# Gated linear attention, a maximum layer and a top-1 expert layer in one kernel: one block's matmuls moved a slice ahead, small copies moved to another queue, preparations and routings moved in the written order

## The chip, the cores and the metric

One core of a Trainium2 chip. The time is that of one execution on the device, in microseconds (us). The engines are named as in the profile: PE (TensorE, matmuls), PEld (its weight loads), DVE (VectorE), ACT (ScalarE), POOL (GpSimd), SP (SyncE, which here only issues DMAs). A name with q (ACTq, SPq) is the engine's sequencer, for example while it issues a DMA.

## The reference

```python
def _attn_ref(q, k, v, alpha):            # 4 batches, 8 heads, 768 steps, head size 48
    for t in range(S):
        state = alpha[:, :, t, :, None] * state + einsum('bhd,bhe->bhde', k[:, :, t], v[:, :, t])
        y[:, :, t] = einsum('bhd,bhde->bhe', q[:, :, t], state)

def _moe_ref(x, w1, w2, w3, w_out):       # x: 3072 x 384, hidden size 768
    h = maximum(maximum(x @ w1, x @ w2), x @ w3)
    return h @ w_out

def _moe2_ref(x, w_gate, w_output_gate, w1, w2):   # 8 experts, hidden size 1024
    e_idx = argmax(x @ w_gate, axis=1)
    for e in range(8):                    # each token goes through one expert
        ye = maximum(x[mask] @ w1[e], 0) @ w2[e]
        out[mask] = gate_w[mask] * sigmoid(x[mask] @ w_output_gate)[:, e] * ye
```

The three functions run one after the other: attention, maximum layer, expert layer.

## The kernel before

**Blocks.** The 3072 tokens are worked in 8 blocks of 384 (two to a batch). A block's attention is cut into 3 chunks of 128 steps and 2 groups b of heads, so 6 attention steps, written (chunk, b). `attend(old, new)` (L276 to L340) does the second half of one step and the first half of the next one. On PE it issues L288 (y from q and the carried state), L297 (transposes of k), L304 (y from the scores A and v), L310 (the update X of the state) and L317 (the scores of the next step). X and y share the one PSUM tile of pool `psY`. DVE then adds X to the state (L325, L327) and masks the scores into A (L338). ACT copies the transposed k (`kn`, L299), scales the next group's state (L330) and copies y into the tile `x32` (L335); only then can the next step's L288 write to `psY`. L304 of that step waits for A.

**Preparation.** Before a block's attention DVE turns its decays into products: `prep_z` (a scan, L191), `prep_k` (L196), `prep_p` (L203 to L208, with a second scan) and `prep_q` (L212), once for each b; one tile Z serves them in turn. `check` and `check_pl` are activations on ACT that look for decays outside the expected range (L175, L177).

**From attention to the maximum layer.** After chunk 2 of b = 1, `finish_x` (L342) moves the fourth head pair's rows to where they belong by six small DMAs from SBUF to SBUF, all issued by ACT. When b = 0 is done too, `split_x` (L348) cuts x into a high and a low part: xH by ACT (L352), xL by DVE (L353), one column block k = 0, 1, 2 after the other. The weights come as packed 64-bit words by SP (`fetch`, L370) and are cut likewise: `cast_a` is three DVE passes (L393, L395, L397), `cast_b` three ACT copies to wH (L405), `cast_c` one DVE subtraction to wL (L409). A cast of number n (0 to 5) makes one slice f = n of 128 hidden columns for the three matrices; n = 6 and 7 make the two halves of the output weights.

**The maximum layer.** `mm1(i, f, w)` (L435) is block i, slice f, matrix w: nine matmuls into one of three PSUM banks of pool `psM`, the products wH·xH, wH·xL and wL·xH for each k. ACT copies the first bank (L444), DVE takes the maximum of the other two (L447, L450), ACT casts the result (L461) and `mm1_lo` takes the low part (L466). `mm2` (L468) is the second product, and `gate_a`, `gate_b` (L411, L419) fold the routing weights into the output weights by transposes (PE), copies (ACT) and small matmuls (PE, then L429 on ACT, L430 on DVE).

**Routing.** `route_a` (L507) finds each token's expert on DVE; `route_b` (L531) counts by two small matmuls, which read its results `oh` and `oc`, into the one bank of pool `psO`; `route_c` and `route_d` (L539, L559) are chains of small DVE operations that read that bank. `mm2` of the blocks from 2 on uses the same bank.

**Order.** Each engine works its own instructions in program order, and that order is written by hand: each `on(t, f, ...)` or `seq(t, dt, ...)` places a function at a time t in units of about one `mm1`, and all are sorted by t. The start (L995 to L1017) is a list with everything up to slice 0 of block 0. Then a list of `steps` places slices of block 0 and block 1 in turn (L1020 to L1044): (0,0), (1,0), (0,1), (1,1), ... with the remaining casts, the gates and block 2's preparation between them. `seq(30, ...)` places block 2's attention among the `mm2` of blocks 0 and 1; block 2's maximum layer begins at 36, block 3's attention at 42, block 4's at 51, block 3's maximum layer at 54. `warm_up(n)` (L950) is n matmuls of a constant that nobody reads. The expert layer follows at the end and is untouched.

Of the kernel before, what the change touches and what calls it, by code (L numbers as in the profile page):

```python
# [88 lines left out]
def _layers(ctx, tc, pool_, wk, K, general, qk, al, a0, v, vT, w123, wout, gates, ew1, ew2, out):  # L89
# [880 lines left out]
    if not general:  # L970
        batches = [(c, b) for c in range(CPB) for b in (1, 0)]

        def last(i, x, y=None):

            def f():
                attend(x and (i, *x), y and (i, *y))
                if x == (2, 1):
                    finish_x(i)
            return (f,)

        def cross(i, x, j, y):

            def f():
                attend((i, *x), (j, *y))
                if x == (2, 1):
                    finish_x(i)
            return (f,)

        def cast_in(n):
# [16 lines left out]
            cross(1, (0, 1), 0, (2, 0)), (warm_up, 4), *ca[:2],  # L1006
            cross(0, (2, 0), 1, (1, 1)), (warm_up, 4), ca[2],
            last(1, (1, 1), (0, 0)), (warm_up, 4), *ch_,
            last(1, (0, 0), (2, 1)), (warm_up, 4), (split_x, 0), cl,
            last(1, (2, 1), (1, 0)), *da[:2], (mm1, 0, 0, 0),  # L1010
            last(1, (1, 0), (2, 0)), da[2], (mm1, 0, 0, 1),
            last(1, (2, 0)), *dh, (mm1, 0, 0, 2), (mm1_lo, 0, 0), (split_x, 1), dl, (load_qkv, 2), (route_consts,))


        steps = []
        for n in (2, 3, 4, 5, 6, 7):
            wa, wh, wl = cast_in(n)  # L1017
# [1 line left out]
            steps += [[[wa[0]], [wa[1]], []], [[wa[2], *nxt, *wh], [wl], []]]
        wa, wh, wl = cast_in(7)  # L1020
        steps[9][2] = [wa[0]]
        steps[10:] = [[[wa[1]], [wa[2], *wh], [(prep_z, 2, 1)]], [[wl], [(prep_k, 2, 1)], [(check_pl, 2), (prep_p, 2, 1)]]]
# [4 lines left out]
        for n, w, fs in ((9, 2, [ga[0]]), (10, 0, [ga[1]]), (10, 1, [gb[0]]), (10, 2, [ga[2], gb[1]]), (11, 0, [gb[2]]),  # L1027
                         (11, 1, [ga[3]]), (11, 2, [ga[4], gb[3]])):
            steps[n][w] = fs + steps[n][w]
        p = []  # L1030
# [245 lines left out]
```

## Time and profile before

| what | value |
|---|---|
| median of 3 runs | 760.96 us (758.26 to 762.04) |
| the profiled execution's own time | 760.24 us |
| its span, first to last instruction | 758.5 us |
| mean granted clock of PE | 0.985 of full |
| instructions | 14575 |

The profiled execution is the one all rows come from. Its own time is 1.7 us above its span, and 0.72 us below the median. Start times in the rows are counted from the start of the span. "Busy" is the time in which an engine has an instruction under way; "idle before" names what ended the wait.

### The profile page before, as it was taken

The numbers are of one execution on the slowest core, as the hardware profiler recorded it, in microseconds if no ns is written. First come the engines' busy times: TensorE is split into PE (matmuls) and PEld (weight loads), VectorE is DVE, ScalarE is ACT, GpSimd is POOL, SyncE is SP. The second block draws the span as 40 slices with busy tenths as digits, with TensorE's granted clock in tenths as the row PEclk, the third lists the DMA queues.
The fourth block names the chain that finished last, engine by engine and source line by source line (L and its number), as shares of the span: only waits on it lengthen the run. The fifth ranks groups of instructions, "written<-read, shape, count | busy, mean of one in ns | idle before, by whom it ended". The sixth has DMA issues, their size and how long they took to land. (4 is left out here: it accounts for less than half of the span.)

```text
span 758.5 us, 14575 instructions
## 1 busy us (share of the span) xinstructions
PE 717.1 (95%) x4782; PEld 637.3 (84%) x4782; DVE 380.8 (50%) x803; ACT 305.9 (40%) x750; POOL 110.6 (15%) x117
## 2 busy tenths in 40 slices
PE   7799999998999999999999999899999999999994
PEld 7688998897999998999999997789975789984672
DVE  7877787468866736637233266411113531111533
ACT  4354433554543524434222234333335553333743
POOL 1000000011021211111111120222222222222211
PEclk9999999999899999999999999999999999999998
DMA  9805210561410412300000041111279631169770
GB/s 265 338 17 177 81 64 1 163 153 46 124 44 28 130 40 55 97 22 10 12 22 9 31 188 32 43 43 44 65 276 336 225 123 40 45 218 385 284 267 23
DMA packets 23741, 86.57 MB, mean 114 GB/s; under 512 B 7988, under 2 KB 11852, under 8 KB 19536
## 3 DMA queue, kind: packets, MB, share of 16 engines
q1 hardware_dynamic: 18192, 73.24, 28.9%
q0 software_dynamic: 3904, 10.84, 4.4%
q10 hardware_dynamic: 1536, 1.18, 0.6%
q8 instruction: 51, 0.84, 0.5%
q14 instruction: 58, 0.48, 0.2%
HBM read 128.09 MB, written 10.63 MB: 183 GB/s over the span
## 5 line engine op out<-in xcount | busy, mean ns | idle before, releaser
L440 PE MATMUL hps<-xH,wH 128*128 128x384 f32 x432 | 151.6, 351 | 1.8 <-ACT xH L352 1.8
L440 PE MATMUL hps<-xH,wL 128*128 128x384 f32 x432 | 146.0, 338 | 0.7 <-DVE wL L409 0.7
L440 PE MATMUL hps<-xL,wH 128*128 128x384 f32 x432 | 146.1, 338 | 0.4 <-DVE xL L353 0.4
L466 POOL TENSOR_TENSOR hL<-hm,hH 128x384 fp32r<-128x384 f32 x36 | 44.8, 1244 | 404.6 <-ACT hH L461 404.5
L895 PE MATMUL psP<-w2H,ch 128*128 128x384 f32 x368 | 100.2, 342 | 2.2 <-ACT ch L855 1.4
L836 PE MATMUL psM<-w1H,cx 128*128 128x512 f32 x276 | 97.0, 406 | 1.7 <-ACTq L1180 1.7
L440 PEld LDWEIGHTS hps<-xH,wH 128*128 128x128 f32 x432 | 82.0, 190 | 8.4 <-ACT xH L352 2.5
L856 DVE SCALAR_TENSOR_TENSOR ch<-psH,ch 128x512 fp32r<-128x512 f32 x46 | 29.7, 686 | 109.2 <-ACT ch L855 108.7
L440 PEld LDWEIGHTS hps<-xL,wH 128*128 128x128 f32 x432 | 82.3, 191 | 0.9 <-DVE xL L353 0.9
L440 PEld LDWEIGHTS hps<-xH,wL 128*128 128x128 f32 x432 | 82.1, 190 | 1.0 <-DVE wL L409 1.0
L895 PEld LDWEIGHTS psP<-w2H,ch 128*128 128x128 f32 x368 | 67.1, 188 | 3.2 <-ACT ch L855 1.6
L476 PE MATMUL ops<-wo,hH 128*128 128x400 f32 x258 | 68.2, 345 | 0.0
L836 PEld LDWEIGHTS psM<-w1H,cx 128*128 128x128 f32 x276 | 52.6, 190 | 15.1 <-ACTq L1180 2.0
L895 PE MATMUL psP<-w2L,ch 128*128 128x384 f32 x184 | 62.1, 337 | 0.0
L915 POOL DMA_INDIRECT out<-yo,sidx x30 | 30.9, 1030 | 204.4 <-ACTq L911 117.2
L447 DVE TENSOR_TENSOR hm<-hm,hps 128x384 f32<-128x384 f32 x48 | 26.5, 551 | 66.4 <-PE hps L440 60.8
L836 PE MATMUL psM<-w1L,cx 128*128 128x512 f32 x138 | 54.9, 398 | 0.1
L461 ACT CAST hH<-hm 128x384 fp32r<-128x384 f32 x43 | 22.0, 512 | 80.8 <-DVE hm L450 77.0
L909 ACT ACTIVATE yo<-psP,xg 128x384 f32<-128x384 f32 x30 | 17.5, 582 | 81.5 <-PE psP L895 60.0
L837 ACT COPY hs<-psM 128x512 f32<-128x512 f32 x46 | 27.0, 588 | 56.7 <-PE psM L836 54.6
L476 PEld LDWEIGHTS ops<-wo,hH 128*128 128x128 f32 x258 | 46.9, 188 | 0.4
L476 PE MATMUL ops<-wo,hL 128*128 128x400 f32 x129 | 44.3, 344 | 0.2 <-POOL hL L466 0.2
(211 smaller groups left out, 1159.3 us busy)
## 6 DMA issues: line engine op xcount, KB each, us to landing
s1a<-in_ew SPq DMA_DIRECT2D x15, 1536.0 KB
s2a<-in_ew SPq DMA_DIRECT2D x15, 1536.0 KB
s1b<-in_ew SPq DMA_DIRECT2D x14, 1536.0 KB
s2b<-in_ew SPq DMA_DIRECT2D x14, 1536.0 KB
ws<-in_w SPq DMA_DIRECT2D x6, 1152.0 KB
at<-in_al SPq DMA_DIRECT2D x16, 336.9 KB
vt<-in_v SPq DMA_DIRECT2D x8, 576.0 KB
x2d<-xs SPq DMA_DIRECT2D x24, 192.0 KB
```

The lines of the kernel that those rows point to most:

```text
L440: mm(ps, slab(a, f)[:, w, k], b[i][:, k], start=(n == 0), stop=(n == 8))
L447: nc.vector.tensor_max(m, m, ps)
L461: nc.scalar.copy(hH[i, f], m)
L466: (nc.gpsimd if not general and i > 1 else nc.vector).tensor_sub(hL[i, f], hps["m"], hH[i, f].bitcast(F32))
L476: mm(ps[:, :DM + NG], a[i, f][:, ts_], wo[f // 3][:, b, f % 3], start=(f + n == 0), stop=(f + n == 7))
L836: mm(ps, cx[j][:, x, ks], w[:, k, fs], start=(k + n == 0), stop=(k + n == 4))
L837: nc.scalar.copy(hs[j][:, fs], ps)
L856: nc.vector.scalar_tensor_tensor(lo, ps, 0.0, hi.bitcast(F32), op0=ALU.max, op1=ALU.subtract)
L895: mm(ps[:, :DM], ch[j][:, x, f * 128:(f + 1) * 128], w[:, f], start=(f + n == 0), stop=(f == NE - 1 and n == 2))
L909: nc.scalar.activation(y, ps[:, :DM], AF.Copy, scale=gate)
L915: nc.gpsimd.indirect_dma_start(out=out[:, :], out_offset=bass.IndirectOffsetOnAxis(ap=sidx[:, j:j + 1], axis=0), in_=y, in_offset=None, bo ...
```

## The change

Four groups of edits. (1) `finish_x` of blocks 0 and 1 issues its six DMAs from SP instead of ACT. (2) `mm1` runs its nine matmuls by kind of product (three wH·xH, three wH·xL, three wL·xH) instead of by k. (3) In the start list four `warm_up(4)` are gone, from the step that follows the first step of block 1 on; the first pass of cast 1 stands two attention steps earlier, its second pass behind `mm1(0,0,1)`, its ACT copies ahead of `mm1(0,0,2)`. After that the slices run (0,1), (1,0), (0,2), (1,1), ... (0,5), (1,4), (1,5), so block 0 is a slice ahead; the casts follow each other every four to five `mm1` instead of every six; the gates and block 2's preparation stand earlier. (4) Block 3's preparation moves ahead: `prep_p` and `prep_q` of b = 1 from 38.3 and 39.3 into block 2's last attention step, b = 0 from 42.6 to 45.0 forward to 37.3 to 43.6. The routings of block 0 (45.6 to 46.8) move to 49.7 to 50.9, that of block 1 from 47.4 to 49.2 to 51.5 to 53.9, with 1.2 units instead of 0.6 between `route_a` and `route_b`.

```diff
     def finish_x(i):
         for c in range(3):
             for h in range(2):
-                nc.scalar.dma_start(out=x32[i][64 * h + D:64 * h + 64, c],
+                (nc.sync if i < 2 else nc.scalar).dma_start(out=x32[i][64 * h + D:64 * h + 64, c],
...
-        for k in range(3):
-            for (a, b) in ((wH, xH), (wH, xL), (wL, xH)):
+        for (a, b) in ((wH, xH), (wH, xL), (wL, xH)):
+            for k in range(3):
...
-            cross(1, (0, 1), 0, (2, 0)), (warm_up, 4), *ca[:2],
-            cross(0, (2, 0), 1, (1, 1)), (warm_up, 4), ca[2],
-            last(1, (1, 1), (0, 0)), (warm_up, 4), *ch_,
-            last(1, (0, 0), (2, 1)), (warm_up, 4), (split_x, 0), cl,
-            last(1, (2, 1), (1, 0)), *da[:2], (mm1, 0, 0, 0),
-            last(1, (1, 0), (2, 0)), da[2], (mm1, 0, 0, 1),
-            last(1, (2, 0)), *dh, (mm1, 0, 0, 2), (mm1_lo, 0, 0), (split_x, 1), dl, (load_qkv, 2), (route_consts,))
+            cross(1, (0, 1), 0, (2, 0)), *ca[:2],
+            cross(0, (2, 0), 1, (1, 1)), ca[2],
+            last(1, (1, 1), (0, 0)), *ch_, da[0],
+            last(1, (0, 0), (2, 1)), (split_x, 0), cl,
+            last(1, (2, 1), (1, 0)), (mm1, 0, 0, 0), (mm1, 0, 0, 1), da[1],
+            last(1, (1, 0), (2, 0)), da[2], *dh, (mm1, 0, 0, 2), (mm1_lo, 0, 0),
+            last(1, (2, 0)), dl, (split_x, 1), (load_qkv, 2), (route_consts,))
...
+        order = [(0, 1), (1, 0)]
+        for f in range(2, 6):
+            order += [(0, f), (1, f - 1)]
+        order.append((1, 5))
+        steps = [[[], [], []] for _ in order]
         for n in (2, 3, 4, 5, 6, 7):
...
+            w0 = {2: 0, 3: 5, 4: 10, 5: 14, 6: 19, 7: 23}[n]
+            for m, x in enumerate(([wa[0]], [wa[1]], [wa[2], *nxt, *wh], [wl])):
+                steps[(w0 + m) // 3][(w0 + m) % 3] += x
...
+        for n, w, fs in ((7, 2, [ga[0]]), (8, 0, [ga[1]]), (8, 1, [gb[0]]), (8, 2, [ga[2], gb[1]]), (9, 0, [gb[2]]),
+                         (9, 1, [ga[3]]), (9, 2, [ga[4], gb[3]]), (10, 0, [gb[4]]), (10, 1, [ga[5]]), (10, 2, [gb[5]])):
             steps[n][w] = fs + steps[n][w]
+        for n, w, x in ((9, 1, (prep_z, 2, 1)), (9, 2, (prep_k, 2, 1)), (10, 0, (check_pl, 2)), (10, 0, (prep_p, 2, 1)),
+                        (10, 2, (prep_q, 2, 1))):
+            steps[n][w].append(x)
...
-            (prep_q, 2, 1), gb[4], ga[5], (mm2, 0, 0, lo), gb[5], last(2, None, (0, 1)), (prep_zk, 2, 0), (mm2, 0, 1, lo),
+            (mm2, 0, 0, lo), last(2, None, (0, 1)), (prep_zk, 2, 0), (mm2, 0, 1, lo),
...
-            (mm2, 1, 2, lo), last(2, (2, 0)), (split_x, 2), (mm2, 1, 2, hi), (route_a, 0))
-        seq(37.3, 1, (check_pl, 3), (prep_p, 3, 1), (prep_q, 3, 1), (check, 3, 1, 0), (check, 3, 1, 1))
-        seq(42.6, 0.6, (prep_z, 3, 0), (prep_k, 3, 0), (check, 3, 0, 0), (prep_pq, 3, 0), (check, 3, 0, 1))
-        seq(45.6, 0.6, (route_b, 0), (route_c, 0), (route_d, 0), (route_a, 1), (route_b, 1), (route_c, 1), (route_d, 1))
+            (mm2, 1, 2, lo), (check_pl, 3), (prep_p, 3, 1), last(2, (2, 0)), (split_x, 2), (mm2, 1, 2, hi), (prep_q, 3, 1),
+            (route_a, 0))
+        seq(37.3, 0.9, (prep_z, 3, 0), (check, 3, 1, 0), (prep_k, 3, 0), (check, 3, 1, 1), (prep_p, 3, 0), (check, 3, 0, 0),
+            (prep_q, 3, 0), (check, 3, 0, 1))
+        seq(49.7, 0.6, (route_b, 0), (route_c, 0), (route_d, 0), (route_a, 1))
+        seq(52.7, 0.6, (route_b, 1), (route_c, 1), (route_d, 1))
```

In the lists `ca`, `ch_`, `cl` are the passes of cast 0 on DVE, on ACT and the last on DVE; `da`, `dh`, `dl` those of cast 1. `last` and `cross` are `attend` within a block and across two, with `finish_x` behind (2, 1).

## Rows read from the trace of the kernel before

**Rows 1.** The page, part 1: PE, busy us, share of the span, instructions.
```profile
PE 717.1 (95%) x4782; PEld 637.3 (84%) x4782; DVE 380.8 (50%) x803; ACT 305.9 (40%) x750; POOL 110.6 (15%) x117
```
**Rows 2.** Stretches: busy us of each engine (instructions), granted PE clock, DMA share, GB/s.
```profile
35.60:39.00 3.40, 3.40 (x28) 3.08 (x23) 2.17 (x5) 1.17 (x4) 0.00 (x0) 0.50 0.14 41
39.00:59.40 20.40, 19.62 (x203) 17.08 (x201) 14.22 (x23) 10.99 (x32) 0.00 (x0) 1.00 0.19 49
62.90:66.30 3.40, 3.40 (x13) 3.40 (x12) 3.33 (x3) 0.58 (x3) 0.00 (x0) 0.50 0.12 45
189.20:196.00 6.80, 6.80 (x40) 6.20 (x39) 5.77 (x18) 2.11 (x7) 0.47 (x1) 0.50 0.01 2
```
**Rows 3.** Waits of PE, 20 to 200 us: total us, times, longest us.
```profile
PE rps L534 <- DVE oh L521: 2.5, 1, 2.5
PE hps L440 <- ACT xH L352: 1.8, 2, 1.6
PE y L288 <- ACT x L335: 1.6, 3, 0.6
PE gps L425 <- ACT wT L417: 1.0, 2, 0.7
...
PE hps L440 <- DVE wL L409: 0.7, 1, 0.7
PE XT L297 <- DVE wo L430: 0.5, 1, 0.5
```
**Rows 4.** Timeline of PE, 34 to 51 us: start, us, instruction, idle before it.
```profile
34.28 0.69 PE L288 MATMUL y<-qt,state 112*112 112x128 f32 x4 [2.89 <-DVE pl L208]
...
36.03 1.23 PE L317 MATMUL sc<-qt,kt 48*128 48x128 f32 x8
...
42.38 0.69 PE L288 MATMUL y<-qt,state 112*112 112x128 f32 x4
...
48.51 0.64 PE L288 MATMUL y<-qt,state 112*112 112x128 f32 x4
...
50.50 0.44 PE L440 MATMUL hps<-xH,wH 128*128 128x384 f32 x1
```
**Rows 5.** Timeline of ACT, 28 to 60 us.
```profile
28.00 4.64 ACTq L345 DMA_DIRECT2D x<-x  x6
...
44.94 0.36 ACT L335 COPY x<-y 112x256 f32<-112x256 f32 x1
...
58.75 1.34 ACT L405 CAST wH<-wu 128x384 fp32r<-128x384 f32 x3
```
**Rows 6.** Timeline of DVE, 28 to 36 us.
```profile
30.86 0.51 DVE L327 TENSOR_TENSOR state<-state,y 48x96 f32<-48x96 f32 x2
...
34.24 0.96 DVE L212 TENSOR_TENSOR qt<-qt,Z 112x768 f32<-112x768 f32 x1
```
**Rows 7.** Groups of DVE instructions, 36 to 118 us: count, busy us, mean ns, idle before.
```profile
L395 DVE SCALAR_TENSOR_TENSOR wu<-ws,wu 128x1152 uint32<-128x1152 uint32 x8 | 10.8, 1354 | 0.1
...
L393 DVE TENSOR_SCALAR wu<-ws 128x1152 uint32<-128x1152 uint32 x8 | 6.0, 756 | 0.0
L450 DVE TENSOR_TENSOR hm<-hm,hps 128x384 f32<-128x384 f32 x11 | 6.0, 549 | 2.1 <-PE hps L440 2.1
...
L338 DVE TENSOR_TENSOR A<-sc,mask 128x512 f32<-128x512 f32 x6 | 4.1, 691 | 0.8 <-PE sc L317 0.6
```
**Rows 8.** Timeline of DVE, 153 to 158 us.
```profile
156.08 0.54 DVE L327 TENSOR_TENSOR state<-state,y 48x96 f32<-48x96 f32 x2 [1.53 <-issue]
```
**Rows 9.** Stretches, columns as in Rows 2.
```profile
184.68:185.66 0.98, 0.98 (x7) 0.88 (x5) 0.84 (x8) 0.00 (x0) 0.00 (x0) 1.00 0.07 17
...
202.98:207.77 4.79, 4.79 (x30) 4.76 (x28) 4.76 (x9) 4.56 (x11) 1.02 (x1) 1.00 1.01 323
203.71:207.68 3.97, 3.97 (x25) 3.97 (x24) 3.94 (x8) 3.92 (x10) 1.02 (x1) 1.00 1.01 313
```
**Rows 10.** Timeline of PE, 205 to 211 us.
```profile
208.81 0.71 PE L317 MATMUL sc<-qt,kt 48*128 48x128 f32 x8
```

More of the change, by code (lines that the diff above doesn't have):

```diff
@@ L344, in finish_x @@
             for h in range(2):
-                nc.scalar.dma_start(out=x32[i][64 * h + D:64 * h + 64, c],
-                                    in_=x32[i][64 * h + 16 * c:64 * h + 16 * c + 16, 3])
+                (nc.sync if i < 2 else nc.scalar).dma_start(out=x32[i][64 * h + D:64 * h + 64, c],
+                                                            in_=x32[i][64 * h + 16 * c:64 * h + 16 * c + 16, 3])
     def split_x(i):
@@ L1005, in _layers @@
             cross(0, (1, 0), 1, (0, 1)), (warm_up, 4), (prep_pq, 1, 0),
-            cross(1, (0, 1), 0, (2, 0)), (warm_up, 4), *ca[:2],
-            cross(0, (2, 0), 1, (1, 1)), (warm_up, 4), ca[2],
-            last(1, (1, 1), (0, 0)), (warm_up, 4), *ch_,
-            last(1, (0, 0), (2, 1)), (warm_up, 4), (split_x, 0), cl,
-            last(1, (2, 1), (1, 0)), *da[:2], (mm1, 0, 0, 0),
-            last(1, (1, 0), (2, 0)), da[2], (mm1, 0, 0, 1),
-            last(1, (2, 0)), *dh, (mm1, 0, 0, 2), (mm1_lo, 0, 0), (split_x, 1), dl, (load_qkv, 2), (route_consts,))
-        steps = []
+            cross(1, (0, 1), 0, (2, 0)), *ca[:2],
[10 more added lines that the diff above has]
+        steps = [[[], [], []] for _ in order]
         for n in (2, 3, 4, 5, 6, 7):
@@ L1018, in _layers @@
             nxt = {2: [(fetch, 5)], 4: [(fetch, 6)], 5: [(fetch, 7)]}.get(n, [])
[L1019 to L1022, printed above, removed]
+            w0 = {2: 0, 3: 5, 4: 10, 5: 14, 6: 19, 7: 23}[n]
+            for m, x in enumerate(([wa[0]], [wa[1]], [wa[2], *nxt, *wh], [wl])):
+                steps[(w0 + m) // 3][(w0 + m) % 3] += x
         for n, b in ((0, 1), (2, 0)):
@@ L1026, in _layers @@
         ga, gb = ([(g, f) for f in range(6)] for g in (gate_a, gate_b))
-        for n, w, fs in ((9, 2, [ga[0]]), (10, 0, [ga[1]]), (10, 1, [gb[0]]), (10, 2, [ga[2], gb[1]]), (11, 0, [gb[2]]),
-                         (11, 1, [ga[3]]), (11, 2, [ga[4], gb[3]])):
+        for n, w, fs in ((7, 2, [ga[0]]), (8, 0, [ga[1]]), (8, 1, [gb[0]]), (8, 2, [ga[2], gb[1]]), (9, 0, [gb[2]]),
+                         (9, 1, [ga[3]]), (9, 2, [ga[4], gb[3]]), (10, 0, [gb[4]]), (10, 1, [ga[5]]), (10, 2, [gb[5]])):
             steps[n][w] = fs + steps[n][w]
+        for n, w, x in ((9, 1, (prep_z, 2, 1)), (9, 2, (prep_k, 2, 1)), (10, 0, (check_pl, 2)), (10, 0, (prep_p, 2, 1)),
+                        (10, 2, (prep_q, 2, 1))):
+            steps[n][w].append(x)
         p = []
-        for n, x in enumerate(steps):
-            f, i = divmod(n, 2)
+        for (i, f), x in zip(order, steps):
             for w in range(3):
-                p += ([] if n == 0 else [(mm1, i, f, w)]) + x[w]
-            if n:
-                p.append((mm1_lo, i, f))
+                p += [(mm1, i, f, w)] + x[w]
+            p.append((mm1_lo, i, f))
         seq(0, 0.1, *p)
```

## The prediction

> **What bounds the kernel now.** I read the page first: PE is busy 95% of the span [rows 1], so other engines matter only where PE waits for them, or where its clock is down. The list of PE's waits names the places between 20 and 200 us [rows 3]; stretches laid over them show the granted clock [rows 2]; the timelines of PE, ACT and DVE show what was late. What lies behind 215 us is not edited.
>
> Three places lose time. (a) In the attention of blocks 0 and 1, PE waited 2.89 us at 34.28 [rows 4]. The row names DVE, but the copy of y was the late one: ACT sat on the six DMA issues of `finish_x(0)` from 28.00 for 4.64 [rows 5]. (b) Around 51 to 62, PE waited 0.7 for wL and up to 1.6 at once for xH of block 1 [rows 3]. (c) At `route_b(1)` it waited 2.5 for `oh` [rows 3]: DVE, which works strictly in order, was behind with preparations and routings, which also held y back for 0.6. Behind each place the clock was at half, 1.2 instead of 2.4 GHz: 35.6 to 39.0, 62.9 to 66.3, 189.2 to 196.0 [rows 2]. Where PE has enough work, a half-clock stretch costs half its length: 1.7, 1.7 and 3.4. The gates add waits of 1.0 and 0.5 [rows 3].
>
> **The change, part by part.**
>
> *Attention of blocks 0 and 1: 2.9 less.* With ACT free, the step now at 34.28 is released when DVE's state add ends (30.86 + 0.51 [rows 6]) and two copies of y of 0.36 each [rows 5] follow: 32.1. The next step hangs on DVE: `prep_q` ends at 34.24 + 0.96 = 35.2 [rows 6], then 0.5 for the state and one copy, 36.1. Then DVE masks (0.69), runs two passes of cast 0 (0.76 + 1.35) [rows 7] and adds the state (0.52): 39.0, with two copies 39.75. Two more steps follow. Such a step now takes from 42.38 [rows 4] to the end of its copy, 44.94 + 0.36 = 45.3 [rows 5], so 2.92. That ends at 45.6, where the trace has 48.51 [rows 4]: 2.9. The four removed `warm_up` are in it; most of them lie beside the wait for y and would save little alone. The copies hide PE's removed work, not the reverse.
>
> Here a rule speaks against the edit. The row shows 4.64 us for six issues. The Trainium skill, "DMA: Bandwidth & Descriptors", section "Issuing engines are not separate DMA queues", says that another issuing engine saves only the sequencer's time to start a DMA, usually small beside the DMA itself. By that the move would bring nothing, the step after that at 34.28 would start at 34.28 + 2.9 = 37.2 instead of 36.1, and the sum would be 1.1 smaller; the trace disagrees, as 4.64 is not small and PE waited behind it.
>
> What SP takes over: twelve issues, at 4.64 / 6 = 0.8 each [rows 5] 9.3 us. In its order they stand behind the five weight fetches and ahead of block 2's loads. DMAs are quiet from 35.6 to 39.0, share 0.14 [rows 2], so the fetches are through, and x of block 0 is not needed before 45.6. I cost it at nothing; what covers it is those 7 us.
>
> *wL of slice 0: 0.6 less.* In the new order of `mm1` six of nine matmuls need no wL, and 0.7 [rows 3] shrinks to about 0.1. The order itself costs nothing: the same matmuls and weight loads. Its bounds are none and 0.6 less.
>
> *x of block 1 against wL of slice 1: 0.5 more, clock unchanged.* The wait of 1.6 goes, as slice 1 of block 0 comes first. But that needs cast 1. By my schedule the first two `mm1` (4.79 / 3 = 1.6 each [rows 9]) begin at 45.6 + 2.0 (a step, 48.51 to 50.50 [rows 4]) = 47.6 and, with the 0.1 of wL, end at 51.0. Behind them DVE has a maximum (0.55), cast pass two (1.35), state (0.52), mask (0.69) and pass three (1.35): 55.5 [rows 6, 7]. ACT copies wH (1.34 [rows 5]): 56.8, and casts hH (a third of that); DVE takes the low part (0.55, as a maximum) and then wL, as wide as the passes (1.35): 59.1. PE gets there with attention (2.0), `mm1` (1.6), the last step (half of one and a bit, 1.2) and six of nine matmuls (1.1) at 56.9. So it waits some 2.1 where it waited 1.6. Bounds: 0 (cast early) and 2.1. A wait of 1.6 put the clock at half [rows 2, 3]; one of 2.1 will likely do so again, so I take the 1.7 as kept.
>
> *Later slices: nothing.* The next casts take DVE 0.76 + 3 x 1.35 = 4.8 us in four to five `mm1` of 1.6, so about 7.5, beside some 2.6 of maxima and low parts (three of 0.55 in each slot of 4.8 [rows 7, 9]). That is nearly all of it, but each wL is due one slot (4.8 us) after its pass. DVE is the cover that could go.
>
> *Gates: 1.3 less.* Waits of 1.0 and 0.5 [rows 3]; with an `mm1` between each copy and its reader I leave 0.2. Bounds 0 and 1.5.
>
> *Block 2's last step: 0.7 more.* `prep_p(3,1)` now stands ahead of the state add at 156.08, in an idle stretch of 1.53 [rows 8]. Its nearest rows: at 32 it lay between the end of the mask (31.37 + 0.69 = 32.06) and `prep_q` at 34.24 [rows 6, 7], 2.2; at 204 it took 3.97 less the 0.96 of `prep_q` [rows 6, 9], 3.0, beside 1.02 of POOL's work. POOL takes part only from block 2's maximum layer on, so here I take 2.2: y, and with it xH and the first `mm1` of block 2, come 0.7 late. Bounds 0 and 1.5.
>
> *Block 3 and the routings: 3.9 less.* The waits of 2.5 and 0.6 [rows 3] and the 3.4 of clock [rows 2] go, because DVE has prepared block 3 before 44 and the routings are not yet due: 6.5. But the routings now stand where block 4 is prepared. There `prep_p, prep_q(4,0)` ends at 207.68 [rows 9] and the scores that read its q begin at 208.81 [rows 10]: 1.1 to spare. New ahead of it stand `route_c(0)` (1.0 [rows 9]), `route_d(0)` (four such operations of six, 0.7) and `route_a(1)` (about twelve, 2.0): 3.7. So PE loses 3.7 - 1.1 = 2.6, part of it at `route_b(1)`, the rest at the scores. Bounds: 0 and, if these chains stretch as `prep_p` does there (3.97 [rows 9]), 5.
>
> Sum: 2.9 + 0.6 - 0.5 + 1.3 - 0.7 + 3.9 = 7.5. From the profiled execution's own 760.24 (span 758.5 and 1.7 around it) that gives **752.7 us**. This execution stands 0.7 below the median of the runs shown, so the drop counted from the median would give 753.5; I keep 752.7.
>
> **The rivals.**
>
> *All waits covered.* Cast 1 is in time, the clock stays up at 60, and the routings fit. For it: DVE's idle time before cast 1's pass two, and routings that are spread over more units. Against it: the in-order sums above. Time: 7.5 + 2.1 + 1.7 + 2.6 = 13.9 less, 746.3.
>
> *VectorE becomes the bound at the routings.* Sums of 3.7 over a slack of 1.1 leave room for the 5 instead of 2.6, and a wait of that size is followed by a half-clock stretch, 1.7 [rows 2]. Time: 752.7 + 2.4 + 1.7 = 756.8. For it: the same kind of wait stands there now [rows 3].
>
> *The clock stays down without the warm-ups: slower.* Between attention steps PE now idles: from my schedule 1.6 us ahead of the step at 36.1, 1.4 ahead of that at 39.8, 0.7 to 0.9 at the others, where 39.0 to 59.4 had PE busy 19.62 of 20.40 at full clock [rows 2]. At half clock the scores took 1.23 [rows 4] instead of 0.71 [rows 10], so a step of 2.0 becomes 3.5. If the clock is down from 34.5 until 59, that is eight steps with 1.5 more and three `mm1` with 1.6 more, 16.8 less about 1 that the copies hide: 752.7 + 15.8 = 768.5. It decides from about 10 us at half clock on; below that I stay faster. Against it: a PE that works at half speed is busier, and the clock came back after 3.4 us at 39.0 and 66.3 [rows 2]. The Trainium skill, "TensorE: Matmul & The Clock Gate", section "A second HAM failure mode: psum-queue depth-cycling", says that frequent short idling between groups of matmuls makes the clock swing; no row here shows such swinging yet, and by that rule this would be the case.
>
> *The move to SP doesn't do what it says.* If the six small DMAs land behind other transfers, x of block 0 is late, each us past 45.6 one us. By the DMA share above, unlikely.
>
> **How the numbers follow.** About 0.5% (3.8 us) is what a measurement of this kernel can tell from no change; so faster means under 757.2, slower over 764.8. Chances: my forecast 0.55; all covered 0.2; VectorE bound at the routings 0.17; clock down 0.05; SP 0.03. The first two are faster; of the third, which lies at the edge, I count 0.04 as faster and 0.13 as the same; the SP case goes to the same. That makes 0.79 faster, 0.16 the same, 0.05 slower. Range: downward all bounds together, 7.5 + 2.1 + 1.7 + 2.6 + 0.7 = 14.6, reach 745.6; upward one half-clock stretch among the attention steps (1.5), 2.4 and 1.7 at the routings reach 758.3. I give 746.0 to 758.0.
>
> **What would show it.** Right: no wait of PE at 34 to 36 over 1.7; block 1's last step begins 2.5 to 3.5 earlier; the wait for xH of block 1 is gone and one for wL of about 2 stands at the first `mm1` of slice 1; no wait over 0.5 at the gates; none at `route_b(1)` over 1, and one of one to two for q of block 4, with full clock around. Wrong: a clock below full over several steps before 50; waits for wL in later slices; a new wait over 3 us at the routings; `split_x(0)` waiting for a DMA.

## The result: 0.95% faster, with a half-clock stretch of 17 us among the attention steps

| | before | changed |
|---|---|---|
| median | 760.68 us (10 runs, 758.14 to 763.60) | 753.86 us (10 runs, 748.88 to 756.70) |
| the profiled execution | 760.24 us, span 758.5, clock 0.985 | 756.70 us, span 754.9, clock 0.981 |

The ratio is 0.9905 [0.988, 0.993] (in brackets the 95% interval): 7.2 us less of 760.68, against 7.5 forecast; the medians stand 6.8 apart. The time lies inside the range forecast. But the profiled run of the changed kernel is its slowest of ten, and its trace shows a reason: what was forecast as 2.9 less in the attention of blocks 0 and 1 came out as 1.8 more. Of all runs below two count as slow, both of E2 (764.17 us, which is its profiled one, and 765.78), and no ratio uses them.

The page's PE line, which answers to [rows 1]; PE has 32 matmul records fewer, eight for each of the four warm-ups:

```profile
PE 715.8 (95%) x4750; PEld 636.3 (84%) x4750; DVE 376.6 (50%) x803; ACT 306.2 (41%) x750; POOL 108.7 (14%) x117
```

The waits of PE in the changed kernel, 20 to 215 us (us in total, times, longest), to be read against [rows 3]:

```profile
PE y L288 <- ACT x L335: 4.9, 8, 1.6
PE hps L440 <- DVE wL L409: 1.7, 1, 1.7
...
PE sc L317 <- DVE qt L212: 0.9, 1, 0.9
PE hps L440 <- ACT xH L352: 0.8, 1, 0.8
PE rps L534 <- DVE oh L521: 0.6, 1, 0.6
PE gps L425 <- ACT wT L417: 0.3, 1, 0.3
PE tps L414 <- DVE wu L397: 0.2, 1, 0.2
```

The waits of 2.9 for y and 2.5 for `oh` are gone, and the 1.0 at the gates is 0.3. In their place: many small waits for the copy of y (4.9 in eight), one of 1.7 for wL, one of 0.9 for q of block 4.

The timeline of PE in the changed kernel (start, us, instruction, wait before it), against [rows 4]. The first rows are the attention steps, each seen by its L288; the rest is one row for each of the later places:

```profile
28.20 0.69 PE L288 MATMUL y<-qt,state 112*112 112x128 f32 x4 [0.51 <-ACT x L335]
...
32.38 0.69 PE L288 MATMUL y<-qt,state 112*112 112x128 f32 x4 [0.82 <-DVE d L203]
...
36.25 0.75 PE L288 MATMUL y<-qt,state 112*112 112x128 f32 x4 [1.59 <-ACT x L335]
...
40.42 1.20 PE L288 MATMUL y<-qt,state 112*112 112x128 f32 x4 [0.54 <-ACT x L335]
...
44.77 1.20 PE L288 MATMUL y<-qt,state 112*112 112x128 f32 x4 [0.27 <-ACT x L335]
...
48.83 1.19 PE L288 MATMUL y<-qt,state 112*112 112x128 f32 x4 [0.36 <-ACT x L335]
...
52.51 1.33 PE L440 MATMUL hps<-xH,wH 128*128 128x384 f32 x3
...
64.54 0.79 PE L440 MATMUL hps<-xH,wL 128*128 128x384 f32 x3 [1.73 <-DVE wL L409]
...
149.89 0.69 PE L288 MATMUL y<-qt,state 112*112 112x128 f32 x4 [1.32 <-ACT x L335]
...
157.79 1.27 PE L440 MATMUL hps<-xH,wH 128*128 128x384 f32 x3 [0.76 <-ACT xH L352]
...
200.65 0.19 PE L534 MATMUL rps<-oh,ut 128*128 128x24 bf16 x1 [0.56 <-DVE oh L521]
...
204.74 0.72 PE L317 MATMUL sc<-qt,kt 48*128 48x128 f32 x8 [0.88 <-DVE qt L212]
```

Stretches of the changed kernel (busy us and instructions of PE, PEld, DVE, ACT, POOL; granted clock; DMA share; GB/s), against [rows 2]:

```profile
28.20:36.70 8.50, 6.09 (x72) 5.20 (x73) 8.34 (x16) 2.93 (x9) 0.00 (x0) 1.00 0.86 343
36.70:53.70 17.00, 15.82 (x113) 12.95 (x112) 10.82 (x18) 7.96 (x23) 0.00 (x0) 0.50 0.02 5
53.70:66.00 12.30, 10.38 (x79) 9.12 (x78) 8.00 (x13) 6.09 (x15) 0.00 (x0) 1.00 0.55 153
190.00:210.00 20.00, 18.06 (x145) 15.77 (x144) 17.46 (x47) 10.54 (x30) 2.06 (x2) 1.00 0.46 135
```

Read both together. The step at 36.25 starts where the forecast put it (36.1): the move of the six DMAs to SP did its work. PE had been busy for 6.09 of 8.50 us up to there; right after it the clock is at 1.2 GHz for 17 us, the L288 row grows from 0.69 to 1.20, and four steps take 16.3 us (36.25 to 52.51). At 64.54 PE waits 1.73 and the clock stays at full, where before it fell after a wait of 1.6. At the routings it is full throughout.

Runs of one kernel differ by 3 to 9 us, so I also use a **ruler** in each profile: how many us after the attention step at about 28 (L288) the first instruction of a stage starts. Nothing before that step was edited. Each row is one profile. The first mark agrees within 0.07 in the nine profiles whose clock is full from that step to there (E1, E5 to E12). The stage between the last two marks, with the same edits in the changed kernel, E1, E5, E8 and E12, takes 49.55 to 50.42, so the last mark can't tell differences under 0.9.

| profile | first `mm1` | first `mm2` | first `mm1` of block 2 | first `mm2` of block 2 | at half clock, 28 to 215 |
|---|---|---|---|---|---|
| before | 22.48 | 95.11 | 130.03 | 183.10 | 3.4, 3.4, 6.8 |
| changed | 24.31 | 94.72 | 129.59 | 179.16 | 17.1 |
| E1 warm-ups back | 19.74 | 89.85 | 124.05 | 173.60 | none |
| E2 `finish_x` on ACT (run of 764.17) | 26.90 | 99.57 | 134.06 | 184.39 | 23.9, 3.4 |
| E3 old order in `mm1` | 21.34 | 95.25 | 129.92 | 180.23 | 6.8, 6.8 |
| E4 before, no warm-ups | 24.42 | 97.03 | 132.68 | 183.46 | 13.7, 3.4 |
| E5 = E1, cast 1 sooner | 19.76 | 88.38 | 122.28 | 172.64 | none |
| E6 = E1, old routings | 19.75 | 89.84 | 123.73 | 173.43 | none |
| E7 = E1, routings earlier still | 19.75 | 89.84 | 123.74 | 177.36 | 6.8 |
| E8 = E1, `finish_x(2)` on SP | 19.76 | 89.86 | 123.16 | 173.58 | none |
| E9 three edits on E1 | 19.74 | 88.36 | 121.66 | 173.06 | 3.4 |
| E10 = E1, old preparation | 19.74 | 89.83 | 123.20 | 173.24 | none |
| E11 before, only the SP move | 19.74 | 92.36 | 127.07 | 178.59 | 3.4 |
| E12 one warm-up back | 19.69 | 89.78 | 123.66 | 174.00 | none |

### The profile page after: what moved, and what is told of

Read it like the earlier page. It is cut to its first block, busy times and chain, and to the rows that moved or that the text cites. A ratio compares the mean times of both kernels' runs of the same rounds, so it can differ in the third digit from the quotient of the medians.

```text
span 754.9 us, 14512 instructions
## 1 busy us (share of the span) xinstructions
PE 715.8 (95%) x4750; PEld 636.3 (84%) x4750; DVE 376.6 (50%) x803; ACT 306.2 (41%) x750; POOL 108.7 (14%) x117
## 5 line engine op out<-in xcount | busy, mean ns | idle before, releaser
L440 PE MATMUL hps<-xH,wH 128*128 128x384 f32 x432 | 104.5, 349 | 0.9 <-ACT xH L352 0.8
L466 POOL TENSOR_TENSOR hL<-hm,hH 128x384 fp32r<-128x384 f32 x36 | 42.9, 1192 | 402.9 <-ACT hH L461 402.9
L440 PE MATMUL hps<-xH,wL 128*128 128x384 f32 x432 | 98.3, 335 | 1.7 <-DVE wL L409 1.7
L440 PE MATMUL hps<-xL,wH 128*128 128x384 f32 x432 | 98.6, 335 | 0.0
L440 PEld LDWEIGHTS hps<-xH,wH 128*128 128x128 f32 x432 | 74.4, 189 | 7.0 <-ACT xH L352 1.5
L440 PEld LDWEIGHTS hps<-xH,wL 128*128 128x128 f32 x432 | 77.0, 188 | 2.0 <-DVE wL L409 2.0
L440 PEld LDWEIGHTS hps<-xL,wH 128*128 128x128 f32 x432 | 77.5, 188 | 0.2 <-DVE xL L353 0.2
```

Source lines behind the costliest of these rows:

```text
L466: (nc.gpsimd if not general and i > 1 else nc.vector).tensor_sub(hL[i, f], hps["m"], hH[i, f].bitcast(F32))
```

## The experiments

Each was timed in five rounds against the kernel before on its chip, and its ratio is to that: E1 to E4 in one job (before: median 758.60), E5 to E8 in a second (759.62), E9 to E12 in a third (758.67). Kernels of different jobs are compared by their ratios. No run takes the order of the slices or the places of the gates back, so what these two edits bring is read from the waits alone.

### E1 to E4: the clock, the SP move, the order in `mm1`

**E1: the four warm-ups back in the changed kernel.**

```diff
-            cross(1, (0, 1), 0, (2, 0)), *ca[:2],
-            cross(0, (2, 0), 1, (1, 1)), ca[2],
-            last(1, (1, 1), (0, 0)), *ch_, da[0],
-            last(1, (0, 0), (2, 1)), (split_x, 0), cl,
+            cross(1, (0, 1), 0, (2, 0)), (warm_up, 4), *ca[:2],
+            cross(0, (2, 0), 1, (1, 1)), (warm_up, 4), ca[2],
+            last(1, (1, 1), (0, 0)), (warm_up, 4), *ch_, da[0],
+            last(1, (0, 0), (2, 1)), (warm_up, 4), (split_x, 0), cl,
```

> The changed kernel with the four warm_up(4) back between the attention steps, all else as changed. Theory A (the idle time between the steps holds PE's clock at half, and at half clock PE sets the length of a step): the clock is full again from about 40 us, slice 0 of block 0 begins some 4 us earlier than in the changed kernel's profile (48 to 49 instead of 52.5), the time is 3 to 5 us under the changed kernel, about 750. Theory B (the copies of y set the length of a step, so PE's filler only adds work): same time or up to 1 us more, 754 to 755, and the steps follow each other every 2.9 to 3.7 us in both.

Measured: 750.20 us (749.00 to 753.16), 0.9889 [0.9865, 0.9914]. Stretches of E1, columns as above:

```profile
28.70:37.20 8.50, 7.18 (x80) 6.17 (x81) 8.34 (x16) 2.92 (x9) 0.00 (x0) 1.00 0.77 307
37.20:54.20 17.00, 16.79 (x181) 14.60 (x180) 12.61 (x22) 8.43 (x24) 0.00 (x0) 1.00 0.05 11
```

And its timeline of PE:

```profile
36.73 0.69 PE L288 MATMUL y<-qt,state 112*112 112x128 f32 x4 [0.51 <-ACT x L335]
...
48.42 0.79 PE L440 MATMUL hps<-xH,wH 128*128 128x384 f32 x3
...
60.13 0.79 PE L440 MATMUL hps<-xH,wL 128*128 128x384 f32 x3 [1.71 <-DVE wL L409]
```

The step at 36.73 is 8.05 behind that at 28.68, exactly as in the changed kernel (36.25 - 28.20): the added matmuls cost nothing, they fill the wait, which shrinks from 1.59 to 0.51. But now the clock stays full and the first `mm1` comes 4.6 us sooner on the ruler. So in these two profiles the missing warm-ups cost 4.6, as theory A has it. The ratios are apart by much less than its 3 to 5 us, and the intervals overlap: the times don't show that the warm-ups are worth anything. A reason shows in the clock of each run: it is 0.981 to 0.995 over the changed kernel's ten runs (mean 0.9897) and 0.992 to 0.997 over E1's six (mean 0.9937). A us at half clock misses half of it, so 0.0103 missing of about 754 us is 15.5 us at half clock in a mean run, and 0.0063 of 750 is 9.5: 6 us more, not 17. By an estimate from the profile's 4.6 us for 17, these 6 us are worth about 1.6, near the 1.2 that the two ratios are apart (0.0016 of 759). So the length of the stretch differs from run to run, and the profile caught a long one.

**E2: `finish_x` of all blocks on ACT again.**

```diff
-                (nc.sync if i < 2 else nc.scalar).dma_start(out=x32[i][64 * h + D:64 * h + 64, c],
+                nc.scalar.dma_start(out=x32[i][64 * h + D:64 * h + 64, c],
```

> The changed kernel with the DMAs of finish_x of blocks 0 and 1 issued by ACT again. My sum: the step that begins at 32.4 begins near 34.3, the one behind it 1.1 us later, and ACT's second set of six issues (about 3.7 us) delays the copies behind slice 0: 1 to 3 us slower than the changed kernel, 755 to 757. Rival (the issue time is small beside the DMA and hidden): the same time, 753 to 754.5.

Measured: 757.27 us (752.23 to 765.78, all twelve runs), 0.9971 [0.9946, 0.9995]; against the changed kernel's ratio 0.0066 of 759, so 5.0 us slower. The old wait is back, in the timelines of ACT and PE of the run of 764.17:

```profile
27.97 4.34 ACTq L345 DMA_DIRECT2D x<-x  x6
```

```profile
33.94 1.19 PE L288 MATMUL y<-qt,state 112*112 112x128 f32 x4 [2.58 <-ACT x L335]
```

More than the 1 to 3 us expected: the wait comes, and with the warm-ups still missing the clock is lower too (mean 0.9862 over the ten runs in the ratio, 0.9897 in the changed kernel).

**E3: the loop over k outside again in `mm1`.**

```diff
-        for (a, b) in ((wH, xH), (wH, xL), (wL, xH)):
-            for k in range(3):
+        for k in range(3):
+            for (a, b) in ((wH, xH), (wH, xL), (wL, xH)):
```

> The changed kernel with mm1's nine matmuls ordered by k again. My sum: wL is needed by the third matmul instead of the seventh, so PE waits about 0.7 us longer for wL of slice 1 (2.4 instead of 1.7), and up to 0.6 for that of slice 0 where the clock is full: 0.7 to 1.3 us slower, about 755. Rival (using the same weights twice in a row is cheaper): every group of nine is shorter, 432 such pairs by up to 10 ns, up to 4 us faster, 750.

Measured: 755.96 us (752.67 to 760.71), 0.9967 [0.9942, 0.9993], 4.7 us above the changed kernel by the ratios. Its timeline of PE, and the stretch behind the second wait:

```profile
50.78 0.44 PE L440 MATMUL hps<-xH,wL 128*128 128x384 f32 x1 [0.68 <-DVE wL L409]
...
61.87 0.69 PE L440 MATMUL hps<-xH,wL 128*128 128x384 f32 x1 [2.42 <-DVE wL L409]
```

```profile
60.70:67.50 6.80, 5.63 (x18) 5.63 (x19) 3.23 (x6) 1.84 (x5) 0.00 (x0) 0.51 0.48 149
```

The order is worth what the prediction put on it in waits: 0.7 at the first slice, 0.7 at the second (2.42 against 1.73). The nine matmuls themselves are no dearer; a matmul follows the last by 0.17 to 0.18 in either order, so weights that stay the same save nothing. What was not expected is that 6.8 us at half clock follow the wait of 2.42. From first `mm1` to first `mm2` the ruler has 73.9 where the changed kernel has 70.4: of these 3.5, 0.7 are the longer wait, and the rest fits half of those 6.8. Over its runs the mean clock is 0.9857 against 0.9897, an estimated 6 us more at half clock; half of that and the two waits of 0.7 make 4.4 of the 4.7.

**E4: the kernel before, less the same four warm-ups.**

```diff
-            cross(1, (0, 1), 0, (2, 0)), (warm_up, 4), *ca[:2],
-            cross(0, (2, 0), 1, (1, 1)), (warm_up, 4), ca[2],
-            last(1, (1, 1), (0, 0)), (warm_up, 4), *ch_,
-            last(1, (0, 0), (2, 1)), (warm_up, 4), (split_x, 0), cl,
+            cross(1, (0, 1), 0, (2, 0)), *ca[:2],
+            cross(0, (2, 0), 1, (1, 1)), ca[2],
+            last(1, (1, 1), (0, 0)), *ch_,
+            last(1, (0, 0), (2, 1)), (split_x, 0), cl,
```

> The kernel before with only the same four warm_up(4) taken out. Theory A: after PE's wait of 2.9 us at 34 the clock stays at half through the attention steps, and slice 0 begins 2 to 4 us later than 50.5: 2 to 5 us slower than before, 763 to 766. Theory B: the warm-ups were 4 to 5 us of PE work of which 1 to 2 us lay on the path: 759 to 760.

Measured: 759.95 us (757.69 to 766.14), 1.0014 [0.9988, 1.004]: no difference that can be told. The mechanism is there all the same, in a stretch of its profile:

```profile
34.00:47.50 13.50, 12.01 (x90) 10.10 (x90) 7.76 (x15) 4.25 (x15) 0.00 (x0) 0.53 0.21 79
```

The clock is at half for 13.7 us where it was for 3.4, and the first `mm1` comes 1.9 later. The mean clock is 0.9799 over its runs and 0.9867 over the 29 runs of before in this job. Theory A's price of 2 to 5 us was too high: the ruler ends only 0.36 later, as this profile has no half clock at the routings. PE waits there as long as before (2.48 at 188.36), and yet the clock stays full:

```profile
191.08 0.19 PE L534 MATMUL rps<-oh,ut 128*128 128x24 bf16 x1 [2.49 <-DVE oh L521]
```

```profile
184.00:196.00 12.00, 8.75 (x77) 7.45 (x77) 11.44 (x34) 4.19 (x14) 0.99 (x1) 1.00 0.07 13
```

So from block 2's first `mm1` to its first `mm2` the order of before takes 50.78 us at full clock, 51.52 with 3.4 us at half (E11) and 53.07 with 6.8 (before).

### E5 to E8: what the later waits are worth (all on E1)

**E5: passes two and three of cast 1, and its last, sooner.**

```diff
-            last(1, (2, 1), (1, 0)), (mm1, 0, 0, 0), (mm1, 0, 0, 1), da[1],
-            last(1, (1, 0), (2, 0)), da[2], *dh, (mm1, 0, 0, 2), (mm1_lo, 0, 0),
-            last(1, (2, 0)), dl, (split_x, 1), (load_qkv, 2), (route_consts,))
+            last(1, (2, 1), (1, 0)), (mm1, 0, 0, 0), da[1], (mm1, 0, 0, 1), da[2],
+            last(1, (1, 0), (2, 0)), *dh, (mm1, 0, 0, 2), dl, (mm1_lo, 0, 0),
+            last(1, (2, 0)), (split_x, 1), (load_qkv, 2), (route_consts,))
```

> The changed kernel with the four warm_up(4) back, and cast 1 sooner: its second pass ahead of mm1(0,0,1), its third ahead of the last but one attention step, its last ahead of mm1_lo(0,0). Theory: PE's wait of 1.7 us for wL of slice 1 came from DVE's order alone, so it shrinks to under 0.3 and the time falls 1.4 to 1.7 us under that of the kernel with the warm-ups (750.2, ratio to before 0.9889), ratio about 0.987. Rival: the last pass waits for ACT's copies of wH, which do not come sooner, and the wait stays over 1 us: the same ratio.

Measured: 749.62 us (748.70 to 755.26), 0.9888 [0.9853, 0.9922]. The wait for wL falls from 1.7 to 0.2; the ruler is 1.5 better at the first `mm2` and 1.0 better at the last mark, little more than that mark can tell. The run times can't tell it from E1.

**E6: the routings at their old places.**

```diff
-        seq(49.7, 0.6, (route_b, 0), (route_c, 0), (route_d, 0), (route_a, 1))
-        seq(52.7, 0.6, (route_b, 1), (route_c, 1), (route_d, 1))
+        seq(45.6, 0.6, (route_b, 0), (route_c, 0), (route_d, 0), (route_a, 1), (route_b, 1), (route_c, 1), (route_d, 1))
```

> The changed kernel with the four warm_up(4) back, and both routings at their places of before (45.6 to 49.2). Theory (it was the early preparation of block 3 that freed DVE, and moving the routings later only made DVE late for block 4): no wait over 0.3 at route_b(1), no wait for q of block 4, 1.3 to 1.7 us under the kernel with the warm-ups, ratio about 0.987. Rival (the routings had to move): the wait of about 2.5 at route_b(1) is back with a half-clock stretch, 2 to 5 us over, ratio 0.992 to 0.996.

Measured: 752.01 us (747.76 to 754.72), 0.9904 [0.9871, 0.9938]. PE waits 1.60 for `oh`, and no longer for q of block 4:

```profile
181.15 0.19 PE L534 MATMUL rps<-oh,ut 128*128 128x24 bf16 x1 [1.60 <-DVE oh L521]
```

So the wait is neither under 0.3, as the theory had it, nor 2.5 with a half-clock stretch, as the rival had it. The ruler ends at 173.43, E1's at 173.60. The later routings trade one wait of 1.6 for waits of 0.5 and 0.9 and gain nothing that can be measured.

**E7: the routings still earlier, 43.7 to 47.5 in the written order.**

```diff
-        seq(49.7, 0.6, (route_b, 0), (route_c, 0), (route_d, 0), (route_a, 1))
-        seq(52.7, 0.6, (route_b, 1), (route_c, 1), (route_d, 1))
+        seq(43.7, 0.4, (route_b, 0), (route_c, 0), (route_d, 0), (route_a, 1))
+        seq(46.7, 0.4, (route_b, 1), (route_c, 1), (route_d, 1))
```

> The changed kernel with the four warm_up(4) back, and the routings earlier still: 43.7 to 44.9 and 46.7 to 47.5. By the same theory DVE has idle time between 43 and 45.4, and the waits at route_b(1) and for q of block 4 go: 1.3 to 1.7 us under the kernel with the warm-ups. Rival: PE waits at route_b or for the maxima of slices 2 and 3 of block 2, as DVE is still busy with block 3's preparation: 0 to 2 us over it.

Measured: 751.76 us (750.37 to 755.20), 0.9907 [0.9878, 0.9936]. Both waits at the routings are gone, but y of block 3 now waits behind the chains on DVE, and a half-clock stretch follows:

```profile
188.46 0.77 PE L288 MATMUL y<-qt,state 112*112 112x128 f32 x4 [2.39 <-ACT x L335]
```

The ruler ends 3.8 worse than E1's; the times can't show it.

**E8: `finish_x(2)` on SP too.**

```diff
-                (nc.sync if i < 2 else nc.scalar).dma_start(out=x32[i][64 * h + D:64 * h + 64, c],
+                (nc.sync if i < 3 else nc.scalar).dma_start(out=x32[i][64 * h + D:64 * h + 64, c],
```

> The changed kernel with the four warm_up(4) back, and finish_x of block 2 issued by SP too. Theory (six issues on ACT hold back its copies wherever they stand): the wait for the copy of y near 150 us, 1.3 in the changed kernel and 0.7 with the warm-ups, goes, 0.5 to 1 us under the kernel with the warm-ups. Rival: SP stands there waiting for a buffer of v until about 147, so x of block 2 lands late and split_x(2) waits: 1 to 4 us over it.

Measured: 749.47 us (747.88 to 751.58), 0.987 [0.9844, 0.9895]. By the times it can't be told from E1 (0.9889). The wait for y in block 2's last steps is gone. With the issues on ACT it goes one to one with the time they took there: 3.81 us and a wait of 0.3 (E6, E7, E12), 3.99 and 0.52 (before), 4.13 and 0.65 (E1), 4.75 and 1.27 (E4), 4.79 and 1.32 (changed). Block 2's first `mm1` is 0.9 sooner than in E1; by the last mark a wait of 1.01 for y at 185 has taken that back (173.58).

### E9 to E12: together, and apart

**E9: E5 and E8 together, with `route_b(0)` to `route_a(1)` at their old place, 45.6, and the rest of block 1's routing from 49.7 on (48.0 before, 52.7 changed).**

```diff
-        seq(49.7, 0.6, (route_b, 0), (route_c, 0), (route_d, 0), (route_a, 1))
-        seq(52.7, 0.6, (route_b, 1), (route_c, 1), (route_d, 1))
+        seq(45.6, 0.6, (route_b, 0), (route_c, 0), (route_d, 0), (route_a, 1))
+        seq(49.7, 0.6, (route_b, 1), (route_c, 1), (route_d, 1))
```

> The changed kernel with the four warm_up(4) back, cast 1 sooner, finish_x of block 2 on SP, and the routing of block 1 split: the routing of block 0 and route_a(1) at 45.6 to 47.4, route_b, c, d(1) at 49.7 to 50.9. Theory (each wait left is an order on DVE or ACT and can be moved into idle time): no wait over 0.3 for wL of slice 1, none over 0.3 at route_b(1), at most 0.6 for q of block 4; from the attention step at 28 us to block 2's first mm2 170.5 to 172 us (179.2 in the changed kernel, 173.6 with the warm-ups); ratio to before 0.984 to 0.986. Rival (DVE and ACT are full there, and a wait removed comes back at the next step): 173 to 174.5 us, ratio 0.987 to 0.989.

Measured: 751.50 us (749.08 to 753.51), 0.9902 [0.9863, 0.9941], no better than E1; the ruler's last mark, 173.06, lies in the rival's 173 to 174.5 and not in the theory's 170.5 to 172. Every wait that was aimed at is gone, and a new one stands in its place. E9's timeline of PE and, behind it, of DVE:

```profile
185.73 0.69 PE L288 MATMUL y<-qt,state 112*112 112x128 f32 x4 [2.79 <-ACT x L335]
```

```profile
178.08 0.17 DVE L511 TENSOR_REDUCE mx<-lg 128x3 f32<-128x24 f32 x1
...
180.35 2.55 DVE L207 TENSOR_TENSOR_SCAN Z<-at,d 112x769 f32<-112x769 f32 x1
...
183.81 0.53 DVE L327 TENSOR_TENSOR state<-state,y 48x96 f32<-48x96 f32 x2
```

From `route_a(1)` at 178.08 through `prep_p` and `prep_q` of block 4 DVE has no gap until the state add at 183.81, and no name on the PE row says so: it names ACT's copy, which is last. DVE is full there, so the waits taken away came back at the next place.

**E10: E1 with block 3's preparation at the places of before, the routings late.**

```diff
-        seq(37.3, 0.9, (prep_z, 3, 0), (check, 3, 1, 0), (prep_k, 3, 0), (check, 3, 1, 1), (prep_p, 3, 0), (check, 3, 0, 0),
-            (prep_q, 3, 0), (check, 3, 0, 1))
+        seq(37.3, 1, (check_pl, 3), (prep_p, 3, 1), (prep_q, 3, 1), (check, 3, 1, 0), (check, 3, 1, 1))
+        seq(42.6, 0.6, (prep_z, 3, 0), (prep_k, 3, 0), (check, 3, 0, 0), (prep_pq, 3, 0), (check, 3, 0, 1))
```

> The changed kernel with the four warm_up(4) back and block 3's preparation at its places of before, the routings at their new ones. My prediction's reason (DVE is free for block 3 and 4 because block 3 is prepared sooner): PE waits again for y near block 3's attention, 0.5 us or more in each of two or three steps, and DVE reaches the routings later, so the wait at route_b(1) grows over 1.5: 1 to 4 us over the kernel with the warm-ups, ratio 0.990 to 0.994. Rival (moving the routings was what removed the wait of 2.5): the same as the kernel with the warm-ups or 0.7 under it, as block 2's last step is not held back: ratio 0.988 to 0.989.

Measured: 753.07 us (750.47 to 754.25), 0.9922 [0.9897, 0.9946]. In the trace the wait for `oh` is 0.54 as in E1 and the ruler ends at 173.24, no worse than E1's. So moving the routings alone takes the 2.5 away, and E6 says that moving the preparation alone leaves 1.6 of it. Of the waits for y that were expected near block 3's attention one came, 0.73 at 175.63. And xH of block 2 is late by 0.2 instead of 0.8, as `prep_p(3,1)` no longer stands ahead of it. The median is 2.9 above E1's in another job, the intervals overlap, and the trace up to 215 us shows no cause for it: whether the sooner preparation is worth anything stays open.

**E11: the kernel before with the one line of E2, the other way round.**

```diff
-                nc.scalar.dma_start(out=x32[i][64 * h + D:64 * h + 64, c],
+                (nc.sync if i < 2 else nc.scalar).dma_start(out=x32[i][64 * h + D:64 * h + 64, c],
```

> The kernel before with one line changed: finish_x of blocks 0 and 1 issued by SP. Theory (that line alone, with the warm-ups kept, gives most of what the first 60 us can give): the step at 34.3 begins near 32.4, the clock stays full after it, the first mm1 of slice 0 begins about 20 us after the step at 28 instead of 22.5, 2 to 3.5 us faster, ratio 0.995 to 0.997. Rival (the skill's rule, only issue time is saved): under 1 us, ratio 0.999 or more.

Measured: 755.68 us (753.74 to 756.78), 0.9952 [0.9928, 0.9976]: 3.6 us less by this line alone, half of what the whole change brought. Its timeline of PE; the first row answers to the step with the wait of 2.89 in [rows 4], the second is the step behind it:

```profile
32.35 0.69 PE L288 MATMUL y<-qt,state 112*112 112x128 f32 x4 [0.81 <-DVE d L203]
...
36.23 0.69 PE L288 MATMUL y<-qt,state 112*112 112x128 f32 x4 [0.50 <-ACT x L335]
```

The first `mm1` is 2.74 sooner. PE still waits 1.60 for xH of block 1 at 58.70, as before, and yet the clock is full from 62 to 66; the same wait was followed by 3.4 us at half in the trace of before. The stage up to the first `mm2` is no shorter for it, 72.62 against 72.63: at 68.37 PE waits 0.93 for a maximum of DVE (L450), a wait that before has not.

**E12: only the first of the four warm-ups back.**

```diff
-            cross(1, (0, 1), 0, (2, 0)), *ca[:2],
+            cross(1, (0, 1), 0, (2, 0)), (warm_up, 4), *ca[:2],
```

> The changed kernel with one of the four warm_up(4) back, that in the longest gap, ahead of the step at 36.2. Theory (the wait of 1.6 there is what drops the clock): the clock is full from 35 to 60, the first mm1 begins 19.5 to 20 us after the step at 28, as with all four; ratio 0.988 to 0.989. Rival (the sum of the gaps drops it): a half-clock stretch among the later steps in this profile or a spread of runs over 5 us; ratio 0.990 or more.

Measured: 751.22 us (748.71 to 753.95), 0.990 [0.9858, 0.9941]; its clock is 0.992 to 0.997 over the runs, as E1's. By its times the rival's signs are there, a spread of 5.2 us and a ratio of 0.990; by the clock of all six runs they are not. A stretch of its profile:

```profile
28.30:54.00 25.70, 21.41 (x235) 18.19 (x236) 21.17 (x37) 11.36 (x33) 0.00 (x0) 1.00 0.31 118
```

Waits of 1.30, 0.78 and 0.88 stand ahead of the next three steps, more than in the changed kernel (0.54, 0.27, 0.36), and the clock holds. So those later gaps don't put the clock down; in these profiles what is filled is the one ahead of the step at 36 (1.59 there, 0.51 here).

## Why the prediction was right, and where its steps were wrong

**Attention of blocks 0 and 1: 2.9 less forecast, 1.8 more in the profile, 2.7 less where the clock holds.** The working in waits and copies was right: step at 36.1 (36.25), end of the attention at 45.6 (45.8 in E1, its 46.44 less the 0.66 by which its step at 28 is later). E11 gives 2.74 for the SP move alone. What was wrong is the sentence "most of them lie beside the wait for y and would save little alone": true of their time, but in that wait they kept PE busy, and I gave their loss a case of 5% instead of a place in the sum. The rival *clock stays down without the warm-ups* came in part, and with it a sign that I had named for being wrong, a clock below full over several steps before 50: the step at 48.51, forecast 2.9 earlier, is 0.3 later in the profile. Its price was too high: it made a step 1.5 longer for each of eight, where here four steps grew by 0.59, 1.14, 1.14 and 1.70 (those of the changed kernel less those of E1), and by the clock of the runs the stretch is shorter in most. That is why 17 us at half clock did not make the kernel slower, past the 10 us from which that rival was to decide. The Trainium skill, "TensorE: Matmul & The Clock Gate", section "A second HAM failure mode: psum-queue depth-cycling", names short idling between groups of matmuls as the cause of a swinging clock. Here the clock did not swing: it fell once behind the wait of 1.59 and stayed down for 17 us with gaps of 0.27 to 0.54, and E12, with gaps of 0.78 to 1.30 at full clock, shows that such gaps alone don't decide.

**The move to SP** did what it says: `split_x(0)` waits for no DMA, and the twelve issues on SP hold up nobody. The rule that I weighed against it (the Trainium skill, "DMA: Bandwidth & Descriptors", section "Issuing engines are not separate DMA queues", by which only a usually small issue time is saved) describes the mechanism but not the size: here that issue time was 3.71 to 4.79 us on ACT for six DMAs, in a chain that PE waited for, and E11 shows 3.6 us.

**wL of slice 0, and x of block 1 against wL of slice 1.** 0.7 went, as forecast. The wait for wL is 1.73 against 2.1. Wrong was "so I take the 1.7 as kept": the clock stays full behind it in the changed kernel and in E1, though it fell behind 2.42 in E3. This error is of the other sign than the one above. But the clock alone does not pay it back: E11 has it full there with the old order, and its stage is as long as before's, as PE then waits 0.93 for DVE. The stage is 2.2 us shorter in the changed kernel and 2.5 in E1, where my terms for it come to 0.9 (0.6, -0.5 and 0.8 of the gates).

**Later slices: nothing.** Right: no wait for wL after slice 1, though DVE was busy 49.13 of the 58 us from 60 to 118, where it had been 47.09.

**Gates: 1.3 less; 1.0 found.** 0.29 and 0.24 are left where 1.5 stood.

**Block 2's last step: 0.7 more; 0.5 found, inside its bounds.** The wait for xH of block 2 went from 0.24 to 0.76. That is the step I named, and E10 confirms it: with `prep_p(3,1)` back at its old place the wait is 0.24. In the profile y at 149.89 waits 1.32 as well, instead of 0.52, and that I missed: the six issues of `finish_x(2)` on ACT hold up the copy of y, and with them on SP (E8) the wait is gone. But it is no cost of the change: E4, with that part of the kernel as before, has 1.27 and E11 0.34, as the issues took 4.75 and 3.82 us. The stage as a whole, 34.92 before, is 34.87, as the gates' wait of 0.53 is gone from it and gate matmuls of 0.73 now stand ahead of it.

**Block 3 and the routings: 3.9 less; 3.5 found** (from block 2's first `mm1` to its first `mm2`: 53.07 before, 49.57 after). The clock is full, and the new waits are 0.56 and 0.20 at `route_b(1)` and 0.88 for q, 1.6 instead of 2.6. But most of the 3.5 is the clock of one profile: the order of before takes 50.78 at full clock (E4), so 2.3 of it are the 6.8 us at half in the trace of before, and 1.2 are left for the edits. My term counted 3.4 of clock as something that the old order always loses, and it costs 2.3 where it is lost. The place was right and the reason only half: I wrote that the 2.5 goes "because DVE has prepared block 3 before 44 and the routings are not yet due". E10 shows that the second does it without the first, E6 that the first without the second leaves 1.6.

Summed by stage, the profile has +1.8, -2.2, -0.05 and -3.5, so 3.9 less up to block 2's `mm2`; E1, with the clock up, has 2.7, 2.5, 0.7 and 3.5 less, 9.5 in all, where my terms gave 7.5. The 7.2 of the ratio lies between the two; by their clocks most runs have less time at half than the profiled one. So the mechanism held for the waits, and that the total came within 0.3 is in part luck: the clock lost among the attention steps, which I had left out of the sum, and the 1.7 that I took as kept at 60 are errors of opposite sign, and the clock at the routings differs from profile to profile.

**A better version.** All versions with the warm-ups back have ratios of 0.987 to 0.9922 with full clock in the attention. The lowest is E8 (0.987 [0.9844, 0.9895]): clearly faster than before, and 0.35% below the changed kernel with intervals that just overlap. The ruler ends 5.6 us sooner, but against the slowest run of the changed kernel, and the lowest of eight ratios is partly chance. That E8 is better than the changed kernel, or than E1, is not shown.

## What to carry to other kernels

Count the issue of small DMAs as work of the issuing engine: six of them, 4.64 us, stood in front of two copies of 0.36 that PE needed, and one line moved them away. The matmuls that nobody reads cost nothing here where they lay in a wait; before such matmuls go, look at what the clock does in the profile without them, and over several runs. On an engine that is full and works in order, a wait that is taken away at one place can come back at the next one, as in E9; a ruler of stage starts shows that where run medians can't. A stage's gain in two profiles can be the clock of one of them: compare it with a second profile of the old order before you give it to the edit.

## What was unexpected of the hardware

The same waits did not bring the same clock. PE's wait of 1.6 for xH was followed by 3.4 us at half in the trace of before and by full clock in E11; 1.73 (changed) and 1.71 (E1) left it full, 2.42 (E3) was followed by 6.8 us at half. The wait of 2.5 for `oh`, with the order of before, was followed by 6.8 us at half (before), by 3.4 (E11) and by full clock (E4). Over the ten runs of one and the same changed kernel the mean clock went from 0.981 to 0.995 and the time, mostly with it, from 756.70 to 748.88. What decides in a given run stays open.

The same six issues of `finish_x(2)` took ACT from 3.81 to 4.79 us, 0.64 to 0.80 each, also where the kernel around them was the same (E4 4.75, before 3.99, E11 3.82), and PE waited by as much more.
